# Streaming a recurrent layer's weights in 384 KB contraction blocks from the inputs, with a new order of groups and smaller buffers, on one Trainium2 core

## Chip, cores, metric

One core of a Trainium2 chip. The metric is device time in microseconds of one execution, as the median of the runs on that core.

The profile's names: PE is TensorE, PEld its weight loads, DVE is VectorE, ACT ScalarE, POOL GpSimd, SP SyncE. A q after a name (SPq) is that engine's instruction queue. L908 is line 908 of the kernel. "t_x<-y" means that t_x is written from y.

## The reference, cut to what matters

Two branches read the same input x of 2048 rows and 640 columns, and a gate mixes them. Branch A is sliding-window attention (32 heads of 20). Branch B is recurrent: 64 segments of 32 rows, each with 8 memory rows that come out of the segment before.

```python
for s in range(n_seg):                      # 64 segments, one after the other
    h = concat([mem, x[:, 32*s:32*s+32]])   # 8 + 32 rows of 640
    q, k, v = h @ Wq, h @ Wk, h @ Wv        # 32 heads of 192: 640 x 6144 each
    p = softmax(where(mask, q @ k.T * 192**-0.5, -1e9))
    o = (p @ v) @ Wo                        # 6144 x 640
    mem = o[:, :8]; outs.append(o[:, 8:])
return g * a + (1 - g) * concat(outs)       # a: branch A, g: sigmoid gate
```

The four weights of branch B are 31 MB in bfloat16. The kernels here find room for some 23 MB of them on chip (46 blocks of 480 KB, or 58 pieces of 384 KB). So a part of them is streamed in every step: it comes from DRAM through a "ring", a few buffers (slots) that are filled and freed in turn. The rest is "resident": loaded once and kept.

## The kernel before

The kernel runs branch A, then what branch B can compute for all segments at once (the projections of each segment's last 8 rows, "tails"), then 64 recurrent steps. In a step the operations are listed by a small scheduler, which simulates their times and emits each engine's instructions in the order of its simulated times. Cuts are marked. In STEP, q0 to v3 are projections of one group of head pairs (a "chunk"), tq and tk their transposes, s scores and softmax, p the transpose of the probabilities (which VectorE spreads into t_PTm), pv the value product, o the output product. x mixes the output of the step before with branch A's rows. Copying a step's memory rows from o into hT, the next step's input, ends the step ("hT eviction").

```python
class Sched:
    LAT = {"PE": 190, "DVE": 125, "ACT": 140, "POOL": 150, "DMA": 2000, "SP": 2000}   # ns after an op's own duration
    # a buffer of tag t may be written when the users of the one made bufs[t] earlier are done
    ...
# buffers of a step: tag: (how many, shape)
"w": (4, [P, 1920]), "tok": (3, [P, 384]), ..., "ga": (1, [SEG, D])          # SEG 32, D 640
STEP = "k0 q0 tk0 k1 tq0 x q1 q2 s0 tk1 tq1 k3 k2 s1 tq2 tk2 q3 p0 tk3 s2 v0 tq3 p1 pv0 s3 v1 o0 p2 pv1 p3 v2 v3 pv2 o1 pv3 o2 o3"

def chunk(kind, s, g):          # one group: 4 head pairs, 20 matmuls of 384 columns
    ...
    ws = [w_of(kind, 4 * g + j, wb[j]) for j in range(4)]     # a block is one head pair, all 640 contraction rows
    for kt in range(KT):
        for j in range(4):
            nc.tensor.matmul(t[32*j:32*j+32, 0:384], lhsT=hT[:, kt, :], rhs=ws[j][:, kt, :], ..., tile_position=(0, 32*j))

def store(s):                   # the "x" of a step: outputs of the step before, mixed with branch A's rows
    f_t:  transpose oT into ox (PSUM)                                          # PE
    ga = sc.buf("ga")
    sc.op("DMA", 500, ... dma_start(ga, ga_dram[s*SEG:(s+1)*SEG, :]), writes=[ga])
    f_r:  ga = ox * (1 - g) + ga                                               # DVE, 32 x 640
    sc.op("DVE", dve(640), f_r, reads=[ox], writes=[ga])
    sc.op("DMA", 500, ... dma_start(outf[s*SEG:(s+1)*SEG, :], ga), reads=[ga])
```

Of 64 weight blocks of 480 KB, 46 stay in SBUF and 18 are copied once into DRAM ("w_packed") and streamed from there every step through the ring "w".

Of the kernel before, what the change touches and what calls it, by code (L numbers as in the profile page):

```python
# [14 lines left out]
SEG = 32  # L15
# [455 lines left out]
KINDS = ("q", "k", "v", "o")  # L471


class Weights:




    def __init__(self, tc, dram, Wq, Wk, Wv, Wo, streamed):
        self.tc, self.nc = tc, tc.nc  # L480
        self.src = {}
        for kind, W in (("q", Wq), ("k", Wk), ("v", Wv)):
            W2 = W.rearrange("(kt p) h e -> p kt (h e)", p=P)
            for pr in range(16):
                self.src[kind, pr] = W2[:, :, pr * 384:(pr + 1) * 384]
        self.Wo = Wo
        self.streamed = streamed
        self.slot = {u: n for n, u in enumerate(streamed)}
        self.packed = dram.tile([len(streamed), P, 1920], BF, name="w_packed")
        self.resident = [(k, 4 * g + i) for k in KINDS for g in range(4) for i in range(4) if (k, 4 * g + i) not in self.slot]  # L490
        self.tiles = {}

    @staticmethod
    def view(kind, t):
        return t.rearrange("p (k c) -> p k c", c=640 if kind == "o" else 384)

    def copy(self, u, dst, engine):
        kind, pr = u
        if kind != "o":
            engine.dma_start(dst, self.src[u])  # L500
            return
        for a in range(2):
            engine.dma_start(dst[64 * a:64 * a + 64, :, :], self.Wo[2 * pr + a].rearrange("(b p) e -> p b e", p=64))

    def load_resident(self, pool, u, engine):
        t = pool.tile([P, 1920], BF, name=f"w_{u[0]}{u[1]}")
        self.copy(u, self.view(u[0], t[:]), engine)
        self.tiles[u] = t

    def pack(self, u, engine):  # L510
        self.copy(u, self.view(u[0], self.packed[self.slot[u]]), engine)

    def get(self, ring, kind, pr):
        u = (kind, pr)
        if u in self.tiles:
            return self.view(kind, self.tiles[u][:])
        t = ring.tile([P, 1920], BF, name="w_ring", tag="w")
        self.nc.sync.dma_start(t[:], self.packed[self.slot[u]])
        return self.view(kind, t[:])


def tail_projections(tc, weights, xTb, xbqk, xbv):

    nc = tc.nc
    nseg = xbqk.shape[0]
    HS = nseg // 2
    with ExitStack() as ctx:
        ring = ctx.enter_context(tc.tile_pool(name="t_ring", bufs=3))
        stage = ctx.enter_context(tc.tile_pool(name="t_stage", bufs=2))
        vst = ctx.enter_context(tc.tile_pool(name="t_v", bufs=3))  # L530
        ps = ctx.enter_context(tc.tile_pool(name="t_ps", bufs=8, space=bass.MemoryType.PSUM))
        n = 0
        for ki, kind in enumerate(("q", "k")):
            for g in range(4):
                ws = [weights.get(ring, kind, 4 * g + i) for i in range(4)]
                for half in range(2):
                    t0 = half * HS * MEM
                    st = stage.tile([P, HS, 12, MEM], BF, name="t_qk")
                    for b2 in range(6):
                        pt = ps.tile([P, 2, HS * MEM], FP32, name="t_psum", tag="ps")  # L540
                        for bb in range(2):
                            i, jj = divmod(2 * b2 + bb, 3)
                            for kt in range(KT):
                                nc.tensor.matmul(pt[:, bb, :], lhsT=ws[i][:, kt, jj * P:(jj + 1) * P],  # L544
                                                 rhs=xTb[:, kt, t0:t0 + HS * MEM], start=(kt == 0), stop=(kt == KT - 1))
                        for bb in range(2):
                            src = pt[:, bb, :].rearrange("p (s t) -> p s t", t=MEM)
                            if n % 2:
                                nc.scalar.copy(st[:, :, 2 * b2 + bb, :], src)
                            else:  # L550
                                nc.vector.tensor_copy(st[:, :, 2 * b2 + bb, :], src)
                        n += 1
                    nc.gpsimd.dma_start(xbqk[half * HS:(half + 1) * HS, :, g, ki, :].rearrange("s p c -> p s c"),
                                      st[:].rearrange("p s b t -> p s (b t)"))
        for pr in range(16):
            w = weights.get(ring, "v", pr)
            for tt in range(4):
                pt = ps.tile([P, 2, 192], FP32, name="t_psv", tag="ps")
                for kt in range(KT):
                    nc.tensor.matmul(pt[:].rearrange("p a d -> p (a d)"), lhsT=xTb[:, kt, tt * P:(tt + 1) * P],  # L560
                                     rhs=w[:, kt, :], start=(kt == 0), stop=(kt == KT - 1))
                vt = vst.tile([P, 2, 192], BF, name="t_vt")
                if n % 2:
                    nc.scalar.copy(vt[:], pt[:])
                else:
                    nc.vector.tensor_copy(vt[:], pt[:])
                n += 1
                nc.gpsimd.dma_start(xbv[2 * pr:2 * pr + 2, tt * P:(tt + 1) * P, :].rearrange("a t d -> t a d"), vt[:])  # L568
# [14 lines left out]
STEP = "k0 q0 tk0 k1 tq0 x q1 q2 s0 tk1 tq1 k3 k2 s1 tq2 tk2 q3 p0 tk3 s2 v0 tq3 p1 pv0 s3 v1 o0 p2 pv1 p3 v2 v3 pv2 o1 pv3 o2 o3"  # L583


def branch_B(ctx, tc, xa_dram, xbqk, xbv, mem0, weights, omg_sb, ga_dram, b_dram, outf):
    nc = tc.nc
    nseg = xa_dram.shape[0]
# [4 lines left out]
        "w": (4, [P, 1920]), "hT": (2, [P, KT, SEG]), "tok": (3, [P, 384]), "vtok": (2, [P, 384]), "K02": (2, [P, 4, 2, L]),  # L593
        "PTm": (2, [P, 2, 4, L]), "PTx": (2, [P, 2, 4, L]), "OT": (2, [P, 3, 4, L]), "Pm": (2, [P, 4, SEG]),
        "xqk": (1, [P, 4, 2, 12, MEM]), "xv": (1, [P, 384]), "ga": (1, [SEG, D]),
    }
    kept = {"QT": (2, [P, 12 * L + 64 - L]), "Kz": (2, [P, 4, 2, L]), "Px": (4, [P, P]), "oT": (1, [P, KT * SEG + P - SEG])}
# [60 lines left out]
    def load_x(s):  # L658
        hb = sc.buf("hT")

        def f():
            nc.gpsimd.dma_start(tile_of(hb)[:].rearrange("p k t -> p (k t)"), xa_dram[s])
        return hb, sc.op("DMA", 500, f, writes=[hb])

    def load_tail(s):
        qk, xv = sc.buf("xqk"), sc.buf("xv")

        def f():
            nc.gpsimd.dma_start(tile_of(qk)[:].rearrange("p g i b t -> p (g i b t)"), xbqk[s].rearrange("p g i c -> p (g i c)"))

        def fv():
            src = xbv.rearrange("(h a) t d -> a h t d", a=2)
            for a in range(2):
                nc.gpsimd.dma_start(tile_of(xv)[:, a * 192:(a + 1) * 192], src[a, :, s * MEM:(s + 1) * MEM, :])
# [4 lines left out]
    def load_w(kind, pr):  # L679
        if (kind, pr) not in weights.slot:  # L680
            return None
        b = sc.buf("w")
        sc.op("SP", 1250, lambda: nc.sync.dma_start(tile_of(b)[:], weights.packed[weights.slot[kind, pr]]), writes=[b])
        return b

    def w_of(kind, pr, b):
        return weights.view(kind, (weights.tiles[kind, pr] if b is None else b["tile"])[:])

    hts = {0: load_x(0)}
    tp, m0 = sc.buf("tr"), sc.buf("ga")  # L690
    sc.op("DMA", 500, lambda: nc.sync.dma_start(tile_of(m0)[0:MEM], mem0), writes=[m0])
# [11 lines left out]
    def chunk(kind, s, g):  # L703
        hT = hts[s][0]
        b = sc.buf("mm")
        wb = [load_w(kind, 4 * g + j) for j in range(4)]

        def f():
            t = tile_of(b, [P, 512], FP32, f"ps_{kind}")
            ws = [w_of(kind, 4 * g + j, wb[j]) for j in range(4)]  # L710
            for kt in range(KT):
                for j in range(4):
                    nc.tensor.matmul(t[32 * j:32 * j + 32, 0:384], lhsT=tile_of(hT)[:, kt, :], rhs=ws[j][:, kt, :],  # L713
                                     start=(kt == 0), stop=(kt == KT - 1), tile_position=(0, 32 * j))
        sc.op("PE", 800, f, reads=[hT] + [w for w in wb if w], writes=[b], name=(kind, s, g), mode=32)
        tok = sc.buf("vtok" if kind == "v" else "tok")
        sc.op("ACT", act(384), lambda: nc.scalar.copy(tile_of(tok)[:], b["tile"][:, 0:384]), reads=[b], writes=[tok])  # L717
        made[kind, s, g] = tok

    def turn(kind, s, g):  # L720
# [3 lines left out]
        def f():  # L724
            t = tile_of(b, [P, 3, P], BF, f"tr_{kind}")
            for k in range(3):
                nc.tensor.transpose(t[:, k, :], tok["tile"][:, k * P:(k + 1) * P], ident[:])  # L727
        sc.op("PE", 170, f, reads=[tok], writes=[b], name=("t" + kind, s, g), mode=128)
# [38 lines left out]
    def scores(s, g):  # L767
# [46 lines left out]
        def f7():  # L814
            dst = tile_of(Px)[:, g * SEG:(g + 1) * SEG].rearrange("p (j t) -> p j t", t=MEM)
# [6 lines left out]
    def turn_p(s, g):  # L822
        Pm, Px = made.pop(("P", s, g))
        PT = sc.buf("tr")

# [226 lines left out]
```

## Time and profile before

| | before |
|---|---|
| median | 2636.82 us (2626.48 to 2647.54, 4 runs) |
| start of the recurrent steps | 597 us |
| one step (median distance of the hT evictions) | 31.5 us |
| weights streamed in a step | 18 x 480 KB |
| DMA share in the steps | 0.87 |

The steps are three quarters of the span and all alike, so what a change is worth is read in a window of some of them. The lines are in the prediction (of waits: engine, line, waited for: us in total, times, longest).

### The profile page before, as it was taken

The numbers are of one execution on the slowest core, as the hardware profiler recorded it, in microseconds if no ns is written. First come the engines' busy times: TensorE is split into PE (matmuls) and PEld (weight loads), VectorE is DVE, ScalarE is ACT, GpSimd is POOL, SyncE is SP. The second block draws the span as 40 slices with busy tenths as digits, with TensorE's granted clock in tenths as the row PEclk, the third lists the DMA queues.
The fourth block names the chain that finished last, engine by engine and source line by source line (L and its number), as shares of the span: only waits on it lengthen the run. The fifth ranks groups of instructions, "written<-read, shape, count | busy, mean of one in ns | idle before, by whom it ended". The sixth has DMA issues, their size and how long they took to land.

```text
span 2629.0 us, 105572 instructions
## 1 busy us (share of the span) xinstructions
PE 2177.0 (83%) x46774; PEld 1540.7 (59%) x46774; DVE 1055.7 (40%) x3266; ACT 941.7 (36%) x1957; POOL 615.3 (23%) x1755
## 2 busy tenths in 40 slices
PE   7888857968888888888888888888888888888887
PEld 6777736835555555555555555555555555556555
DVE  4666632323333333333434333333334344333333
ACT  3555532213333333333333333333333333333333
POOL 3111112363222222222222222222222222222221
PEclk7777768998999999999999999999999999999999
DMA  4333248738888888888888888888888888889886
GB/s 139 92 92 92 87 93 192 167 126 271 295 283 295 292 292 296 291 300 297 301 293 302 291 312 291 299 295 299 307 298 300 291 302 302 281 303 310 302 306 234
DMA packets 234613, 670.93 MB, mean 255 GB/s; under 512 B 34058, under 2 KB 68498, under 8 KB 234146
## 3 DMA queue, kind: packets, MB, share of 16 engines
q1 hardware_dynamic: 207906, 603.86, 67.9%
q0 software_dynamic: 26240, 60.23, 8.5%
q8 instruction: 368, 6.03, 0.9%
q14 instruction: 99, 0.81, 0.1%
HBM read 634.60 MB, written 38.22 MB: 256 GB/s over the span
## 4 chain that ended last, share of the span: by engine, by line
PE 49%; DMA 38%; issue 6%; ACT 3%; DVE 2%; POOL 1%; SPq 0%; POOLq 0%; ACTq 0%; DVEq 0%
DMA t_w<-w_packed 35%; PE ps_o L876 11%; PE ps_v L713 7%; PE ps_k L713 7%; PE qk_ps L132 4%; PE ps_q L713 4%; PE ps_pv L852 4%; PE t_psum L544 4%; ACT pt L220 2%; PE s_ps L217 2%; DMA w_ring<-w_packed 1%; PE tr_q L727 1%; POOL xbv L568 1%; PE S_ps L781 1%; PE out_ps L189 1%
## 5 line engine op out<-in xcount | busy, mean ns | idle before, releaser
L713 PEld LDWEIGHTS <-t_hT 128*32 128x32 bf16 x15360 | 410.4, 99 | 538.0 <-issue 351.6
L713 PE MATMUL ps_v<-t_w,t_hT 128*32 128x384 bf16 x1920 | 300.2, 335 | 136.1 <-DMA t_w<-w_packed 135.2
L876 PE MATMUL ps_o<-t_OT,w_o 128*128 128x40 bf16 x11520 | 336.1, 180 | 34.9 <-issue 34.9
L876 PEld LDWEIGHTS <-w_o 128*128 128x128 bf16 x11520 | 308.9, 96 | 71.0 <-issue 56.7
L713 PE MATMUL ps_v<-w_v,t_hT 128*32 128x384 bf16 x3200 | 308.6, 339 | 0.0
L713 PE MATMUL ps_k<-w_k,t_hT 128*32 128x384 bf16 x3840 | 285.9, 348 | 26.3 <-DVE t_hT L885 17.5
L713 PE MATMUL ps_q<-t_w,t_hT 128*32 128x384 bf16 x1280 | 265.6, 344 | 47.7 <-DMA t_w<-w_packed 47.0
L713 PE MATMUL ps_k<-t_w,t_hT 128*32 128x384 bf16 x1280 | 269.4, 347 | 24.3 <-DMA t_w<-w_packed 22.0
L713 PE MATMUL ps_q<-w_q,t_hT 128*32 128x384 bf16 x3840 | 278.4, 346 | 0.0
L885 DVE CAST t_hT<-ps_o 128x40 bf16<-128x40 f32 x63 | 12.6, 199 | 639.7 <-PE ps_o L876 639.7
L717 ACT CAST t_vtok<-ps_v 128x384 bf16<-128x384 f32 x256 | 123.0, 481 | 345.1 <-PE ps_v L713 345.0
L220 ACT ACTIVATE pt<-s_ps 128x1024 bf16<-128x1024 f32 x180 | 180.9, 1024 | 127.4 <-PE s_ps L217 127.3
L857 ACT CAST t_OT<-ps_pv 128x480 bf16<-128x480 f32 x256 | 143.1, 559 | 222.1 <-PE ps_pv L852 218.9
L717 ACT CAST t_tok<-ps_k 128x384 bf16<-128x384 f32 x256 | 122.7, 479 | 214.5 <-PE ps_k L713 213.9
L717 ACT CAST t_tok<-ps_q 128x384 bf16<-128x384 f32 x256 | 122.7, 479 | 207.5 <-PE ps_q L713 205.1
L791 DVE TENSOR_REDUCE sm_mx<-S_ps 128x4 f32<-128x160 f32 x256 | 82.3, 321 | 230.0 <-PE S_ps L781 230.0
L876 PE MATMUL ps_o<-t_OT,t_w 128*128 128x40 bf16 x3840 | 140.8, 180 | 40.6 <-issue 29.4
L835 DVE TENSOR_TENSOR t_PTx<-PT_ps,mk_x 128x320 bf16<-128x320 f32 x256 | 125.1, 489 | 98.6 <-PE PT_ps L830 98.0
L759 POOL COPY t_K<-t_xqk 128x64 bf16<-128x64 bf16 x256 | 60.7, 237 | 407.9 <-DMA t_xqk<-xbqk 120.0
L222 DVE TENSOR_TENSOR pt<-pt,pat 128x1024 bf16<-128x1024 bf16 x180 | 124.3, 691 | 73.8 <-ACT pt L220 71.1
L750 DVE COPY t_K<-tr_k 128x256 bf16<-128x256 bf16 x256 | 72.0, 281 | 190.4 <-PE tr_k L727 190.3
L852 PE MATMUL ps_pv<-t_PTx,t_xv 128*64 128x160 bf16 x1536 | 147.1, 245 | 0.6 <-issue 0.6
(134 smaller groups left out, 3833.9 us busy)
## 6 DMA issues: line engine op xcount, KB each, us to landing
t_w<-w_packed SPq DMA_DIRECT2D x1152, 480.0 KB, 5.2
xbqk<-t_qk POOLq DMA_DIRECT2D x16, 768.0 KB, 8.1
t_xqk<-xbqk POOLq DMA_DIRECT2D x64, 192.0 KB, 5.1
w_ring<-w_packed SPq DMA_DIRECT2D x14, 480.0 KB, 5.2
xbv<-t_vt POOLq DMA_DIRECT2D x64, 96.0 KB, 2.1
t_xv<-xbv POOLq DMA_DIRECT2D x128, 48.0 KB, 5.0
w_q<-in_B_Wq_dram SPq DMA_DIRECT2D x12, 480.0 KB, 5.2
w_k<-in_B_Wk_dram SPq DMA_DIRECT2D x12, 480.0 KB, 5.5
```

The lines of the kernel that those rows point to most:

```text
L132: nc.tensor.matmul(pst[:, gg, :], lhsT=Wp[:, kt, 4 * g:4 * g + 4, :].rearrange("p h d -> p (h d)"), rhs=stt['xT'][:, kt, :], start=(kt == ...
L220: nc.scalar.activation(out=pt, in_=sp[:], func=ACT.Exp, scale=scale)
L222: nc.vector.tensor_tensor(out=pt, in0=pt, in1=pat.unsqueeze(1).to_broadcast([P, 2, 512]), op=ALU.min)
L544: nc.tensor.matmul(pt[:, bb, :], lhsT=ws[i][:, kt, jj * P:(jj + 1) * P], rhs=xTb[:, kt, t0:t0 + HS * MEM], start=(kt == 0), stop=(kt == KT ...
L713: nc.tensor.matmul(t[32 * j:32 * j + 32, 0:384], lhsT=tile_of(hT)[:, kt, :], rhs=ws[j][:, kt, :], start=(kt == 0), stop=(kt == KT - 1), ti ...
L717: sc.op("ACT", act(384), lambda: nc.scalar.copy(tile_of(tok)[:], b["tile"][:, 0:384]), reads=[b], writes=[tok])
L750: nc.vector.tensor_copy(tile_of(K02)[:, :, :, 0:SEG], src)
L791: nc.vector.tensor_reduce(out=x["mx"][:], in_=view(), axis=AX.X, op=ALU.max)
L835: nc.vector.tensor_tensor(out=tile_of(dst)[:], in0=PT["tile"][:, i, :, :].unsqueeze(2).to_broadcast([P, 2, 4, L]), in1=mk[:].unsqueeze(1). ...
L852: nc.tensor.matmul(t[64 * a:64 * a + 64, 160 * b:160 * b + 160], lhsT=v[:, c:c + 64], rhs=p["tile"][:, a, :, :].rearrange("p j l -> p (j l ...
L857: sc.op("ACT", act(480), lambda: nc.scalar.copy(tile_of(OT)[:].rearrange("p b j l -> p (b j l)"), o["tile"][:, 0:480]), reads=[o], writes= ...
L876: nc.tensor.matmul(t[:, dt * L:(dt + 1) * L], lhsT=w[:, b, dt * P:(dt + 1) * P], rhs=OT["tile"][:, b, i, :], start=(g == 0 and i == 0 and ...
```

## The change

Its intent: shorten the time that a ring slot is taken, even out when streamed weights are due, and cut some PE and VectorE work. Weights are cut into 80 pieces of 384 KB; a projection piece is one block of 128 contraction rows for all four head pairs of a group. 22 of them are streamed a step, straight from the input tensors, through a ring of 5, and are taken last in their group. Transposes work on 64 columns, the 8 tail keys meet 16 queries instead of 40, and the groups come in a new order. SBUF is full, so smaller things were squeezed; one of them is "ga".

```diff
-        "w": (4, [P, 1920]), ... "ga": (1, [SEG, D]),
+        "w": (RING, [P, PIECE]), ... "ga": (1, [SEG, D // 2]),          # RING 5, PIECE 1536
+    def order(self, kind, g):                       # the streamed contraction blocks come last
+        return sorted(range(5), key=lambda m: (kind, g, m) in self.streamed)
@@ chunk
-            for kt in range(KT):
-                for j in range(4):
-                    nc.tensor.matmul(..., rhs=ws[j][:, kt, :], ...)
+            for x, kt in enumerate(weights.order(kind, g)):
+                w = w_of(kind, g, kt, wb)
+                for j in range(4):
+                    nc.tensor.matmul(..., rhs=w[:, j * 384:(j + 1) * 384], ...)
@@ order of a step
-STEP = "k0 q0 tk0 k1 tq0 x q1 q2 s0 ... pv2 o1 pv3 o2 o3"
+STEP = "q0 k1 tq0 q1 k0 tq1 tk1 k2 tk0 q3 s0 s1 v0 q2 tk2 v1 tq2 p0 k3 p1 s2 tq3 pv0 tk3 v2 pv1 s3 x p2 v3 o0 p3 pv2 o1 pv3 o2 o3"
@@ store
-        ga = sc.buf("ga")
-        load ga (640 columns); f_r over 640 columns; store ga
+        for h in range(2):
+            ga, c = sc.buf("ga"), h * D // 2
+            load ga (columns c to c + 320); f_r over 320 columns; store ga
@@ ... turn (64-column transposes), turn_p / values (16 queries for tail keys), tail_projections,
@@ ... one DRAM tensor xin for x and tails, resident loads in three batches: cut
```

## The prediction

> **What bounds the kernel now.** I began with the page's head: which engine is busiest, what the 40 slices look like, what the last chain is made of.
>
> ```profile
> PE 2177.0 (83%) x46774; PEld 1540.7 (59%) x46774; DVE 1055.7 (40%) x3266; ACT 941.7 (36%) x1957; POOL 615.3 (23%) x1755
> ...
> DMA  4333248738888888888888888888888888889886
> ...
> q1 hardware_dynamic: 207906, 603.86, 67.9%
> ...
> PE 49%; DMA 38%; issue 6%; ACT 3%; DVE 2%; POOL 1%; SPq 0%; POOLq 0%; ACTq 0%; DVEq 0%
> ...
> t_w<-w_packed SPq DMA_DIRECT2D x1152, 480.0 KB, 5.2
> ```
>
> The DMA row shows three stages: branch A up to about slice 6 (364 us), the tail projections up to 597 us, and then 64 recurrent steps at a steady 8 tenths. VectorE and ScalarE are at 40% and below everywhere. The chain alternates between PE and one transfer, the streamed weights: 1152 of them, 18 a step, 480 KB each, 5.2 us from issue to landing. The last stage is 2029 us, 31.7 us a step (the hT evictions in the trace lie 31.5 us apart in the median), so it decides. I then asked for a steady window and for the waits in it.
>
> ```profile
> 1000.00:1500.00 500.00, 419.39 (x10011) 285.01 (x10007) 187.84 (x649) 170.90 (x391) 112.18 (x362) 0.96 0.87 295
> ...
> PE ps_v L713 <- DMA t_w<-w_packed: 31.4, 46, 1.8
> ...
> PE ps_o L876 <- issue: 23.1, 14, 2.6
> ...
> SPq L683 <- PE ps_v L713: 100.8, 62, 3.0
> SPq L683 <- PE ps_o L876: 87.7, 48, 3.8
> ```
>
> Columns of the first line: length, busy PE, PEld, DVE, ACT, POOL, granted clock, DMA share, GB/s. PE is idle 81 us of 500, 5.1 us a step; the DMA engines are idle 13%. Neither is full, because each waits for the other: PE waits for a block to land (PE stood still 55 us before instructions on t_w), and the queue that loads blocks waits for PE to release a ring slot (the SPq lines). So the step is bound by a ring of four slots: 4 slots x 31.5 us = 126 slot-us, of which 18 x 5.2 = 94 are transfers under way, and 32, or 1.8 us a block, are slots that hold a landed block. That is long because a block is one head pair's whole contraction, and the chunk's loop takes four blocks in turn from its first matmul to its last: a streamed block stops the chunk at its start and is held to its end.
>
> Two floors under a step. **DMA:** 439 engine-us a step in the packet records, over 16 engines 27.4 us; 93% of it is weight packets of 3840 B, 2304 a step at a mean of 179 ns (median 149). **PE:** adding unstalled start-to-start times from the trace (a projection chunk 929 ns, or 870 each for a pair; an output group 1600; scores 434; values 538; a transpose with its switch 180 to 270) over the step's order gives 24.0 us.
>
> The stage ahead of it has its own waits:
>
> ```profile
> 376.26 34.48 DMA w_ring<-w_packed
> 410.88 98.03 PE t_psum L544 x881
> ...
> 540.00:560.00 20.00, 16.50 (x93) 9.03 (x93) 5.13 (x10) 4.70 (x10) 12.98 (x19) 1.00 0.27 91
> ```
>
> PE stands still from 364 to 411 us, while its first streamed block queues behind the resident weights that GpSimd loads in one burst (DMA share 1.0 from 380 to 420). Then query and key tails run back to back. From 513 to 595 the value tails go at the pace of 64 small stores issued by GpSimd (0.71 us plus gaps each, 82 us), not of PE, whose 320 matmuls of 384 columns need 51 us.
>
> **What the Trainium skill says.** *TensorEngine Tiling (Array Packing)*, Key Properties: changing the tiling mode drains TensorE. The trace agrees: a chunk followed by another chunk takes 812 ns, followed by another mode 929. *Runtime: NRT & Kernel Launch*, Instruction fetch mechanics: instructions arrive in 16 KiB blocks of 256, mostly hidden. The block size agrees (q8: 368 packets, 6.03 MB); the hiding does not quite: in the output groups PE stops about 2.1 us in most steps with nothing to wait for ("issue" above), and in the two such stops I compared the stop ended 1.5 us after a 16 KiB packet did. *DMA: Bandwidth & Descriptors*, Latency and other measured facts: row pitches of 512 KiB and larger powers of two lose bandwidth. The new source rows lie 12,288 B apart (outputs 3840 B), far from that; no run of this case shows such reads of 3 KB yet. Same page, Specifications: full rate needs at least 512 B a transfer; 3072 B is above it, and the 3072 B packets in the trace (the tail queries and keys) have a median of 121 ns, 25.4 GB/s an engine against 25.8 at 3840 B.
>
> **The change, part by part.**
>
> *Bytes.* 22 pieces of 384 KB in place of 18 blocks of 480 KB: 8.65 MB against 8.85 MB a step, 2.2% less. In engine time it is about nothing: 2816 packets x (121 + the 24 to 30 ns by which the mean exceeds the median) = 408 to 425 us, against 409. With the other 30 us the DMA floor stays at 27.4 to 28.4 us. So fewer bytes are not the gain.
>
> *Streamed piece last, ring of 5.* The same 1920 KB of ring. A piece is one contraction block for all four column groups, used by the last 4 (or 8) of a chunk's 20 matmuls: the wait moves from the chunk's first matmul to its last fifth, and the hold after landing falls from 0.7 to 0.9 us plus waiting to about 0.2 us plus waiting. I laid the 22 uses on the unstalled PE time of the new order: 2, 3, 4, 5, 7, 8, 9, 10, 12, 14, 16, 17, 19, 21, 22 pieces are used by 0.8, 2.8, 3.5, 4.9, 6.1, 7.9, 8.7, 9.9, 11.3, 13.7, 16.0, 17.6, 19.9, 22.0 and 23.3 us. An even supply over 23.5 us is never off by more than 1.5 pieces, less than a ring of 5 evens out. So transfers can run nearly without a break. A hold of about 1 us a piece leaves over 4 slots under way, 1.6 MB; at the observed shortest landing of 3.1 us about 1.06 MB saturates. I put the DMA share at 95% (before: 87%; the quarter of 5 us windows that are best before have 94% or more): 27.7 / 0.95 = 29.1 us a step.
>
> *PE.* Values: six of twelve 160-column matmuls shrink to 64 columns, some 110 ns less per group, 0.44 us a step. Transposes of 64 columns are twice as many, but pair up beside each other and take about the old 180 ns; they, and the probabilities' transposes, now share the mode of scores and values, yet the count of mode switches in the order only falls from 25 to 24. About 0.1 us. PE floor: 23.5 us. All of this lies beside the transfers, so alone it is worth nothing. 56 more PE instructions a step (112,016 rows in the program against 108,432) mean no more fetch stops than one a step.
>
> *DVE.* The tail spread on half the partitions and 128 columns instead of 320 saves perhaps 0.25 us x 4; off the path.
>
> *Before the steps.* No packing of streamed blocks into DRAM in branch A, but 33 instead of 27 resident loads there; branch A is not bound by transfers (share 0.31 to 0.42), so 0. Tail projections: late weights go in turn on the SP queue, a few at a time, so the first piece lands some 5 us after SP gets there at 376: start at 382 instead of 411. Queries and keys: same matmuls, 103 us. Value stores alternate between GpSimd and ScalarE, with 4 buffers: 64 x 0.88 = 57 us instead of 82. Then the 15 us or so of landing and constants as before: 382 + 103 + 5 + 57 + 15 = 562 us, 35 less than 597.
>
> *Sum.* 562 + 64 x 29.1 + 4 of ending = 2428; I say 2430 us, 7.8% less than 2635.
>
> **The rivals.** (a) *Transfers are hidden by nothing and already full:* if 87% is the practical ceiling, because some engines lag or packets from the strided inputs take longer than from packed DRAM, the step stays at 31 to 32 us and only the tail's 35 us are won: 2590 to 2650. For it: the mean packet is already 20% over its median, and 3 KB rows at a pitch are untried here. Against: single 5 us windows at 97%, and the SPq waits, which show that the queue waits for slots. (b) *PE becomes the bound:* 23.5 us clean, plus a 2 us fetch stop, plus waits for evictions in the new order, would be 26 to 27 us, 2250 to 2300 in all. For it: the PE chain is 49% now. Against: the DMA floor lies above it, so it needs packets faster than 179 ns by more than their size. (c) *Bursts bring the waits back:* eight groups take two pieces; if each first piece waits for the second and the fetch stop freezes the ring, the share gains only half, 91%, and the step is 30.4: 2512.
>
> **Range and chances.** Share 97% with cheap packets: 27.4 / 0.97 = 28.2 a step, 2371; share 92% with dear packets: 28.2 / 0.92 = 30.6, 2524. The start may miss by 20 us either way. Hence 2350 to 2530. Slower needs costly strided reads (3%); within 2% needs rival (a) (6%); faster by over 2%, below 2583, 91%.
>
> **What would show it.** Right: DMA share 0.93 to 0.97 in the steps, above 310 GB/s; 28 to 30 us between hT evictions; PE still waiting for t_w, but late in its chunks; mean 3072 B packet 143 to 152 ns; steps starting at about 560 us; the value stores no longer ahead of PE in the chain. Wrong: mean packets of 165 ns or more (strided reads cost), the share still at 0.88 (slots are not what it lacks), or a chain dominated by PE and ACT (rival b).

## More of the kernel before

Waits between 1000 and 1500 us (engine, line, waited for: us in total, times, longest).

```profile
DVE t_ga L908 <- PE ox_ps L901: 15.1, 16, 1.5
...
POOL t_ga L905 <- DMA out_dram<-t_ga: 1.1, 1, 1.1
```

The mix of a step's output with branch A's rows (t_ga) waits only for PE's transpose, 1 us a step. Its rows had been loaded before that.

## The result

The changed kernel takes 2730.09 us (2727.5 to 2739.79, 4 runs) against 2636.82 us: slower, ratio 1.036 with a 95% interval of 1.031 to 1.041. Ratios here are the mean of one kernel's runs over the mean of the other's runs of the same rounds, so they are not quite the ratio of the medians quoted.

The page of the changed kernel, same lines as for the kernel before:

```profile
PE 2090.3 (77%) x48566; PEld 1569.8 (58%) x48566; DVE 1051.0 (39%) x3330; ACT 923.3 (34%) x1957; POOL 579.8 (21%) x1752
...
DMA  3211165688788777788888788888777878888876
...
DMA 47%; PE 27%; issue 7%; POOL 3%; DVE 2%; SPq 0%; POOLq 0%; DVEq 0%; ACT 0%; ACTq 0%
DMA t_w<-in_B_Wq_dram 13%; DMA t_ga<-ga_dram 10%; DMA out_dram<-t_ga 10%; PE ps_o L917 9%; DMA t_w<-in_B_Wv_dram 8%; DMA t_w<-in_B_Wk_dram 5%; PE ps_q L728 5%; PE t_psum L548 4%; PE ps_v L728 3%; PE ps_pv L889 2%; PE ps_k L728 1%; DVE t_PTm L873 1%; POOL b_Kz L785 1%; PE S_ps L805 1%; POOL b_QT L764 1%
```

No engine is fuller than before, and the DMA row shows fewer eights, not more. New in the chain are two small transfers, the load of branch A's rows and the store of the output: a fifth of the span. The window 1000 to 1500 us of the changed kernel (columns as in the prediction: the clock is the third number from the end, then DMA share and GB/s):

```profile
1000.00:1500.00 500.00, 377.80 (x9945) 277.93 (x9948) 179.45 (x643) 159.42 (x374) 113.35 (x360) 0.89 0.81 275
```

PE is idle 122 us of 500 instead of 81, the DMA share fell from 0.87 to 0.81, and a step takes 33.9 us instead of 31.5. The granted clock fell too, from 0.96 to 0.89; e1 below says what that is worth. The waits of this window:

```profile
DVE t_ga L952 <- DMA t_ga<-ga_dram: 119.4, 15, 9.5
...
PE ps_pv L889 <- DVE t_PTm L873: 86.0, 15, 7.0
...
POOL t_ga L949 <- DMA out_dram<-t_ga: 53.2, 17, 4.5
```

VectorE waits 8 us in each step for rows of branch A, and PE waits 5.7 us in each step for t_PTm, which VectorE makes. How the two hang together is in the chain, in order of time (start, length, what):

```profile
1514.81 3.69 DMA out_dram<-t_ga
1518.51 0.28 issue
1518.79 5.42 DMA t_ga<-ga_dram
...
1524.30 0.13 DVE t_ga L952
...
1524.77 0.48 DVE t_PTm L873
...
1525.29 0.61 PE ps_pv L889 x6
```

There is one half-width buffer. The first half is mixed and stored, 3.7 us; only then may the second half be loaded into the same buffer, 5.4 us; only then can the second mix run. The scheduler counted each transfer as 500 + 2000 ns, 5 us for the two, and placed the second mix just ahead of the last group's t_PTm. VectorE takes its instructions in that order (in all 63 such steps of the trace t_PTm comes right after the second mix), so t_PTm, whose own input had been ready since about 1516.6 us, stood behind it until 1524.8. In order of time (start, length, what, and in brackets the idle time before it):

```profile
1516.38 0.19 PE L860 MATMUL PT_ps<-ident,b_Px 128*64 128x32 bf16 x1
...
1524.30 0.54 DVE L952 SCALAR_TENSOR_TENSOR t_ga<-ox_ps,omg_sb,t_ga 32x320 bf16<-32x320 bf16 x1 [8.20 <-DMA t_ga<-ga_dram]
1524.77 0.47 DVE L873 TENSOR_TENSOR t_PTm<-PT_ps,mk_m 128x320 bf16<-128x320 f32 x1
```

PE's value product for the last group and the output groups o2 and o3 stood behind t_PTm, and with them the ring slots that those would have freed. The transfers ran dry: the queue that loads weights waited 156 us of 500 for output groups (88 before, the prediction's last line of waits).

```profile
SPq L493 <- PE ps_o L917: 155.6, 46, 8.7
```

The start did come out as hoped. The chain of the changed kernel ahead of the steps:

```profile
374.28 4.30 DMA w_ring<-in_B_Wq_dram
378.72 105.10 PE t_psum L548 x934
...
554.49 1.79 PE ps_q L728 x20
```

The steps begin at 554 us instead of 597.

### The profile page after: what moved, and what is told of

Its sections match the earlier page's. It is cut to its first block, busy times and chain, and to the rows that moved or that the text cites. A ratio compares the mean times of both kernels' runs of the same rounds, so it can differ in the third digit from the quotient of the medians.

```text
span 2725.9 us, 109560 instructions
## 1 busy us (share of the span) xinstructions
PE 2090.3 (77%) x48566; PEld 1569.8 (58%) x48566; DVE 1051.0 (39%) x3330; ACT 923.3 (34%) x1957; POOL 579.8 (21%) x1752
## 4 chain that ended last, share of the span: by engine, by line
DMA 47%; PE 27%; issue 7%; POOL 3%; DVE 2%; SPq 0%; POOLq 0%; DVEq 0%; ACT 0%; ACTq 0%
DMA t_w<-in_B_Wq_dram 13%; DMA t_ga<-ga_dram 10%; DMA out_dram<-t_ga 10%; PE ps_o L917 9%; DMA t_w<-in_B_Wv_dram 8%; DMA t_w<-in_B_Wk_dram 5%; PE ps_q L728 5%; PE t_psum L548 4%; PE ps_v L728 3%; PE ps_pv L889 2%; PE ps_k L728 1%; DVE t_PTm L873 1%; POOL b_Kz L785 1%; PE S_ps L805 1%; POOL b_QT L764 1%
## 5 line engine op out<-in xcount | busy, mean ns | idle before, releaser
L889 PE MATMUL ps_pv<-t_PTm,t_vtok 128*64 128x160 bf16 x1536 | 117.5, 261 | 382.9 <-DVE t_PTm L873 382.9
L889 PEld LDWEIGHTS <-t_vtok 128*64 128x64 bf16 x1536 | 73.7, 120 | 395.8 <-issue 393.4
L952 DVE SCALAR_TENSOR_TENSOR t_ga<-ox_ps,omg_sb,t_ga 32x320 bf16<-32x320 bf16 x128 | 68.4, 534 | 517.0 <-DMA t_ga<-ga_dram 511.3
L728 PE MATMUL ps_q<-w_q,t_hT 128*32 128x384 bf16 x3584 | 199.5, 338 | 18.8 <-DVE t_hT L927 18.4
L728 PE MATMUL ps_k<-w_k,t_hT 128*32 128x384 bf16 x4096 | 212.9, 328 | 0.0
L728 PE MATMUL ps_v<-w_v,t_hT 128*32 128x384 bf16 x3584 | 195.5, 332 | 0.1
L751 PEld LDWEIGHTS <-t_tok 128*64 128x64 bf16 x3072 | 103.7, 110 | 104.1 <-issue 38.9
L917 PEld LDWEIGHTS <-t_w 128*128 128x128 bf16 x4608 | 151.7, 103 | 10.8 <-issue 9.4
L873 DVE TENSOR_TENSOR t_PTm<-PT_ps,mk_m 128x320 bf16<-128x320 f32 x256 | 122.9, 480 | 80.9 <-PE PT_ps L860 77.1
L728 PE MATMUL ps_q<-t_w,t_hT 128*32 128x384 bf16 x1536 | 119.6, 330 | 43.8 <-DMA t_w<-in_B_Wq_dram 42.8
```

The costliest lines, as they stand in the source:

```text
L728: nc.tensor.matmul(t[32 * j:32 * j + 32, 0:384], lhsT=tile_of(hT)[:, kt, :], rhs=w[:, j * 384:(j + 1) * 384], start=(x == 0), stop=(x == K ...
L751: nc.tensor.transpose(t[64 * a:64 * a + 64, k, :], tok["tile"][:, c:c + 64], ident[:], tile_position=(0, 64 * a))
L873: nc.vector.tensor_tensor(out=tile_of(PTm)[:], in0=src.to_broadcast([P, 2, 4, L]), in1=mk_m[:].unsqueeze(1).unsqueeze(3).to_broadcast([P, ...
L889: nc.tensor.matmul(t[64 * a:64 * a + 64, 160 * b:160 * b + 160], lhsT=V["tile"][:, c:c + 64], rhs=PTm["tile"][:, a, :, :].rearrange("p j l ...
L917: nc.tensor.matmul(t[:, dt * L:(dt + 1) * L], lhsT=w_of("o", g, m, wb)[:, c:c + P], rhs=OT["tile"][:, b, i, :], start=(g == 0 and n == 0), ...
```

## The experiments

Eleven kernels ran, three rounds each, beside the kernel before on the same chip. Every one gave a correct result. "e1" is also the base for e4 to e11.

**e1: the second half no longer waits for the first half's store.** Two half-width buffers do not fit: a build of the changed kernel with them is turned down, with 0.5 KB a partition left where the last pool wants 0.625 (a message of the build, not a run). But the rows use 32 partitions only, so the second half can lie on partitions 32 to 63 of the same columns. The transposed output is there already: each transpose takes 128 columns of oT in steps of 32, so partitions 32 to 63 hold the next block.

```diff
-"ga": (1, [SEG, D // 2])
+"ga": (1, [2 * SEG, D // 2])
+        loads = [load ga[32*h:32*h+32] for h in range(2)]          # both at once
         for h in range(2):
-            f_r: ga = ox[0:32][:, 320*h : 320*h+320] * omg + ga
+            f_r: ga[32*h:32*h+32] = ox[32*h:32*h+32][:, 192*h : 192*h+320] * omg[32*h:32*h+32] + ga[32*h:32*h+32]
```

> The changed kernel, with the two halves of a step's branch A rows in one 64-partition tile (first half on partitions 0 to 31, second on 32 to 63, same 640 bytes a partition), so that the second half no longer waits for the first half's store. All else as in the changed kernel. Theory A (the single half-width buffer makes store, load and the second mix follow one another, the mix stands at the head of VectorE's queue and PE's value product waits behind it, 86 us of 500 or 5.7 us a step): the wait for t_ga falls from 8 us a step to under 1, the step from 33.9 to 28 to 29.5 us, the total to 2350 to 2450 us. Theory B (the new sources, pieces or order cost the time, and VectorE merely shows it): total stays above 2650 us, and PE's waits move to t_w.

Measured: 2393.28 us (2384.82 to 2400.46), ratio to before 0.907 (0.901 to 0.913). Theory A's numbers hold; theory B is out. The window and the waits of e1:

```profile
1000.00:1500.00 500.00, 429.89 (x11363) 303.62 (x11357) 209.45 (x734) 182.88 (x428) 128.10 (x412) 0.96 0.93 313
```

```profile
DVE t_ga L954 <- issue: 0.2, 1, 0.2
```

The wait for the rows is gone (0.2 us in 500), no wait of PE for t_PTm is left in the list, the DMA share is 0.93 and a step takes 28.4 us in the median, 28.7 in the mean. The whole difference between slower by 3.6% and faster by 9.3% is this one buffer: 337 us, or 5.3 us a step.

One rival is a slower TensorE: the granted clock is 0.89 in the changed kernel's window, 0.96 in e1's and 0.96 before. But by the profile PE's busy time is 25.6 us a step in the changed kernel and 24.7 in e1 (377.80 and 429.89 of 500 us), so the clock can account for at most 0.9 of the 5.2 us between the two steps. And it came back with the buffer alone, so here it goes along with PE's waiting. What lowers it no run shows.

**e2: only the place of x undone.** The change had also moved x to late in the step, right ahead of the last value products.

```diff
-... k0 tq1 tk1 k2 tk0 ... pv1 s3 x p2 ...
+... k0 tq1 tk1 x k2 tk0 ... pv1 s3 p2 ...
```

> The changed kernel with only the output transpose x moved back to an early place of the step, after the second key transpose; the single half-width buffer stays. Theory A: the chain of store, load and second mix is as long as before and stalls VectorE near the start of the step instead, so the total stays at 2650 to 2780 us. Theory C (it is the late place of x, ahead of the last value product, that hurts, and an early place has slack): total 2380 to 2500 us.

Measured: 2876.06 us (2868.29 to 2883.15), ratio 1.092. Theory C falls: early is worse. A (no gain) is right in kind but its range was too low by 100 us. Waits of e2 in the same window:

```profile
ACT S_ps L821 <- DVE S_ps L818: 113.1, 16, 10.2
DVE t_ga L952 <- DMA t_ga<-ga_dram: 103.3, 14, 9.0
```

The wait is about as long, 7.4 us each time, and now stands ahead of the first groups' softmax: ScalarE's part of it (S_ps) waits for VectorE's, up to 10.2 us. A step takes 36.2 us.

**e3: the half-width buffer put into the kernel before.**

```diff
-"ga": (1, [SEG, D])         # one load, one mix, one store
+"ga": (1, [SEG, D // 2])    # load, mix, store, then load, mix, store
```

> The kernel before with only the half-width single buffer for branch A's rows and the mix in two halves taken over from the change. Theory A: VectorE waits some 5 to 8 us a step for the second half; the kernel before has no slack for all of it, so it slows by 2 to 6 us a step: 2750 to 3000 us. Theory B: same as before, 2620 to 2660 us.

Measured: 2954.53 us (2935.61 to 2963.11), ratio 1.120, in A's range. (As in the change, the first memory rows are then loaded through "w", once, before the steps.) The same pair of waits appears in a kernel that has none of the rest of the change:

```profile
DVE t_ga L910 <- DMA t_ga<-ga_dram: 93.3, 14, 8.4
POOL t_ga L907 <- DMA out_dram<-t_ga: 57.8, 24, 4.5
...
PE tr_k L727 <- DVE t_ga L910: 51.3, 14, 5.1
```

Here it is a key transpose on PE that waits for the mix, 3.7 us each time. So the buffer is enough to cause the loss, and e1 shows that without its chain there is none.

**e4: e1 with x early.** The edit of e2 on top of e1.

> e1 with x moved to the early place as well. Theory A: with the chain gone the place of x matters little: within 1% of e1. Theory C: faster than e1 by more than 2%.

Measured: 2408.78 us (2403.21 to 2420.91), ratio 0.915 beside 0.907: within 1%. With the chain gone, the place of x matters little.

The next seven ask where e1's gain comes from.

**e5: the streamed pieces first in their group.**

```diff
-sorted(range(5), key=lambda m: (kind, g, m) in self.streamed)
+sorted(range(5), key=lambda m: (kind, g, m) not in self.streamed)
```

> e1 (2393 us) with the streamed pieces used first in each group instead of last; same pieces, ring and order of groups. Theory D (using them last is what shortens the hold of a ring slot and lets the DMA share rise from 0.87 to 0.94): each piece is held about 0.6 us longer, the share falls to 0.89 to 0.91 and the step grows by 1 to 1.6 us: 2455 to 2500 us. Theory E (ring of 5 and small pieces do it alone): within 1% of e1.

Measured: 2393.28 us (2389.26 to 2409.04), ratio 0.910. No difference, so theory D falls on this point and E holds. From the issues and landings of the weight loads in the traces one can take how long a slot is taken after its piece has landed (landing to the next issue into the same slot): 1.84 us before, 1.30 in e1, 1.23 in e5. First or last, a projection's contraction block is read by four matmuls that follow one another. In projection groups with one streamed block, the first and the last matmul that read it start 0.66 us apart before, and 0.01 us apart in e1 and in e5 (medians). So the place is not what shortens the hold. The shape of the piece fits it, but no run changes the shape alone, and the hold also moves with order and ring: 1.53 in e6 and 0.99 in e7, with the same pieces.

**e6: the old order of the groups.** STEP of the kernel before in e1.

> e1 with the order of the groups in a step taken from the kernel before. Theory D': the new order spreads the uses evenly; in the old one four pieces are due in the two value chunks that follow one another, so the share falls a little: 2410 to 2450 us. Theory E': order is worth under 1%.

Measured: 2483.83 us (2479.7 to 2489.8), ratio 0.943: 91 us slower than e1, more than D' expected (57 at most). The hold is 1.53 us, the step 29.8 us in the mean, the DMA share of the window 0.91:

```profile
1000.00:1500.00 500.00, 422.95 (x11081) 301.92 (x11073) 192.44 (x704) 178.60 (x416) 125.95 (x401) 0.94 0.91 308
```

(Which pieces are streamed was left as it is, chosen for the new order. The old order also has x early, which alone cost 15 us in e4.)

**e7: a ring of 4.** `RING = 5` becomes `RING = 4`.

> e1 with a ring of 4 pieces instead of 5 (1536 KB under way or held instead of 1920). Theory D (ring slots bound the transfers): step 29.5 to 30.5 us, 2440 to 2510 us, DMA share about 0.89. Theory F (the engines themselves are the limit at 0.94): within 1% of e1.

Measured: 2576.05 us (2572.87 to 2590.47), ratio 0.979. The largest single loss, larger than D expected:

```profile
1000.00:1500.00 500.00, 407.69 (x10433) 283.89 (x10426) 195.47 (x687) 169.40 (x397) 117.27 (x380) 0.95 0.88 289
```

Slots under way (mean time from issue to landing over the mean distance of issues) are 3.3 in e7 and 4.0 in e1, 1.3 and 1.6 MB. The ring bounds the transfers. With four slots the step is 31.5 us in the mean, as before the change (31.6, with four larger slots): without the fifth slot, smaller pieces, new order and less work on PE and VectorE together do not make the steps shorter.

**e8: a ring of 4, and the 3 KB it frees used for one more resident piece,** 21 streamed.

```diff
-RING = 5;  LAST = 6;  STREAMED "q": (2, 1, 1, 2)
+RING = 4;  LAST = 7;  STREAMED "q": (2, 1, 1, 1)
```

> e7 with the freed 3 KB a partition given to one more resident piece: 21 streamed pieces a step instead of 22, 4.3% fewer bytes. Theory D: the loss of the slot and the gain of the bytes cancel, within 1.5% of e1. Theory F: about 4% less in the steps than e1, some 2320 us.

Measured: 2501.15 us (2468.83 to 2505.53), ratio 0.945. Neither: 4.5% slower than e1. The fewer bytes are worth 75 us against e7, the slot 183.

**e9: 128-column transposes back.**

```diff
-for a in range(2): transpose(t[64*a:64*a+64, k, :], tok[:, 64 columns], tile_position=(0, 64*a))
+transpose(t[:, k, :], tok[:, 128 columns])
```

> e1 with the three transposes of 128 columns per group back in place of the six of 64. Theory G (PE has slack, the transfers set the step): a few tenths of a us more PE time a step from more mode switches, hidden: within 1% of e1 (2393 us). Theory H (the narrower transposes carry part of the gain): 1 to 3% slower than e1.

Measured: 2391.73 us (2384.71 to 2402.74), ratio 0.907. G holds: the narrower transposes are worth nothing here.

**e10: the streamed pieces from a packed copy** in DRAM, as the kernel before did it.

```diff
+units += [copy piece u into w_packed[slot of u] for u in streamed]     # once, during branch A
-nc.sync.dma_start(tile, inputs' rows of the piece)
+nc.sync.dma_start(tile, w_packed[slot of u])
```

> e1 with the streamed pieces copied once during branch A into a DRAM tensor, 384 KB contiguous each, and streamed from there, instead of 3 KB rows 12 KB apart in the inputs. Theory I (pitch does not matter): mean packet 140 to 145 ns, total within 1% of e1. Theory K (strided rows cost part of the bandwidth): mean packet below 135 ns and over 2% faster.

Measured: 2398.43 us (2391.49 to 2415.85), ratio 0.909; mean 3072-byte packet over the steps 141 ns, as in e1 (141). Reading 3 KB rows 12 KB apart costs nothing that these runs show; the packing could be dropped for free.

**e11: a sixth slot for one resident piece,** 23 streamed.

```diff
-RING = 5;  LAST = 6;  STREAMED "k": (1, 0, 1, 2)
+RING = 6;  LAST = 5;  STREAMED "k": (1, 1, 1, 2)
```

> e1 with one resident piece given up for a sixth ring slot: 23 pieces a step, 4.5% more weight bytes. Theory D (slots): from ring 4 to 5 the share went from 0.887 to 0.937; a sixth slot gives 0.95 to 0.96, engine time 450 us a step, so 29.2 to 29.6 us a step, 2420 to 2455 us. Rival: slots are worth more than bytes even here, share 0.975 and more, total at or below e1.

Measured: 2388.71 us (2372.66 to 2390.38), ratio 0.905 (0.899 to 0.910), beside 0.907 for e1 in other rounds: no difference that these runs show. The total is the rival's (at or below e1), the share, 0.955 over the steps, is D's. What D had wrong is the cost: 435 engine-us a step instead of 450, because a packet took 137 ns in the mean.

```profile
1000.00:1500.00 500.00, 430.86 (x11734) 309.18 (x11734) 214.25 (x751) 186.88 (x439) 132.54 (x423) 0.98 0.95 337
```

4.5% more weight bytes at that share give the same step (28.5 us in the mean, 28.7 in e1): here slots and bytes balance.

## Why the prediction was wrong

**The step that failed: a part of the change that the sum left out.** "The change, part by part" lists bytes, ring, PE, DVE and the start, and of VectorE it says "off the path". The halved "ga" is in the diff and in none of these lists, nor in a rival. What the runs put in that gap is a term of +5.3 us a step (2730 - 2393 = 337 us over 64 steps), made of a store of 3.7 us and a load of 5.4 us in a row ahead of a mix, less the slack. Removing it (e1) and adding it to the old kernel (e3) both show it. The chain could have been seen: one buffer, used twice in a step, with a store between the uses. Where it hurts is in the order that the scheduler emits: the second mix comes 7 instructions after the first on VectorE, ahead of work that PE needs. The prediction gave "slower" 3%, and only for strided reads. The prediction asked of the weight ring how long each slot is held, and did not ask it of the other buffers whose size the diff changed.

**The sum for the rest.** 2428 was worked out for a kernel without that term; e1, which is that kernel, takes 2393. By terms: DMA share predicted 0.95, measured 0.937 over e1's steps; weight packets predicted at 145 to 151 ns, measured 141; DMA floor predicted 27.7, measured 26.9 us (431 engine-us a step over 16); step predicted 29.1, measured 28.7 us; start of the steps predicted 562, measured 554. The share was too high and the packets too dear, so the step came out closer than its terms. In the changed kernel itself the share was 0.81, below even the mark named for a wrong prediction ("the share still at 0.88"), but with another cause than the one given beside it: slots were still what transfers lacked, only now because PE stood still.

**Bytes are not the gain:** as it happened, weight packets take 398 engine-us a step in e1 against 411.

**"Used last" was given part of the credit wrongly.** The prediction let the hold fall because the piece is used last, and the wait moves to the last fifth of the chunk. e5 shows no effect of the place (2393 both ways). The other half of that sentence, four successive matmuls a piece, may have mattered; it was not tried alone.

**Ring and order carry the steps' gain.** The slots arithmetic balances: before, 5.17 us to land and 1.84 us held in 4 slots give 31.5 us for 18 blocks; in e1, 5.23 and 1.30 in 5 slots give 28.7 for 22 pieces. That is bookkeeping and would balance for any kernel. What was forecast is a hold of about 1 us and over 4 slots under way; measured are 1.30 us and 4.0. The prediction's "1.06 MB saturates" was an estimate (the shortest landing, 3.1 us, at 16 engines' 3840 B in 179 ns), and e7 speaks against it: 1.3 MB under way, share 0.887. Of the 243 us between before and e1, 46 lie ahead of the first hT eviction (at 628.9 us before, 582.9 in e1), 91 go when the old order is put back (e6), and some 106 are left for smaller pieces, a fifth slot and all else together. These are not shares that add up: taking the fifth slot away costs 183 us by itself (e7), nearly all of the 197 won in the steps, so what the slot and the order give overlaps. How much is due to the smaller piece was not tried.

**PE and transposes:** "alone it is worth nothing" held for the transposes (e9). The narrower tail keys were not tried alone.

**Rivals.** (a), full transfers: out, 0.955 was reached. Its other leg, dear strided reads: out by e10. (b), PE as the bound: not seen. (c), bursts with a 91% share: e6, the old order, has that share, but no run shows bursts as its cause. None of them was what happened in the changed kernel. One reading was too wide: VectorE and ScalarE are at 40% or below over the whole span, but not everywhere: in branch A, from 0 to 300 us, they are 55 to 66% and 44 to 59% busy. Nothing in the sum rests on it.

**The start:** right in kind, 43 us won instead of 35. The first streamed piece landed at 378.6 us; query and key tails took 105 us; the value tails some 67 us (484 to 551) instead of 57, less than the 82 before. Two errors offset each other here: the value tails took 10 us more, and the 5 + 15 us allowed around them for landing and constants were about 3. The mark "value stores no longer ahead of PE" did not come: their issues by GpSimd, with idle time between them, still make the chain from 496 to 551 us.

## What to carry to other kernels

When a diff halves a buffer and doubles its uses, write down the chain store, load, use for it as for the big transfers, with landing times from the trace (here 3.7 + 5.4 us for 20 KB each), and look at what stands behind the use in its engine's queue: an engine at 39% busy set the step's length. A scheduler that orders a queue by assumed latencies can put such a use too early when it assumes too little (5 us here against 9.1); no run tried the order that true latencies give. For a streamed ring, compare slots x period with (landing + hold) x pieces; here a fifth slot was worth more than 4.3% fewer bytes (e8), and a sixth, paid for with 4.5% more bytes, changed nothing. Whether smaller pieces help by themselves is open.

## What the Trainium skill lacked or had wrong

- *DMA: Bandwidth & Descriptors*, Anatomy of one DMA, gives about 2.0 us plus the bytes' time for a transfer issued by GpSimd, by that fit, as an estimate, 2.05 us for 20 KB. (The page says elsewhere that the fixed part is smaller when HBM is lightly loaded.) With the DMA engines 81% busy, 20 KB stores and loads took 3.7 and 5.4 us in the chain shown, and loads and stores of t_ga 3.5 us in the median, 5.9 at most; in e1, at 93%, 4.7 in the median.
- No page says how many bytes must be under way to fill the engines. Here, with pieces of 384 KB, rings of 4, 5 and 6 gave shares of 0.887, 0.937 and 0.955 over the steps.
- *DMA: Bandwidth & Descriptors*, Latency and other measured facts, has row pitches from 512 KiB up. 3 KB rows at a pitch of 12,288 bytes ran as fast as contiguous ones (141 ns a packet in e1 and in e10).
- No page has that the mean time of a packet moves with the ring: 147 ns with a ring of 4, 141 with 5, 137 with 6, with the same median of 121 ns. More bytes under way cannot be the whole of it: the changed kernel, ring of 5, has 3.3 slots under way, as e7 has, and 143 ns. No run settles why.
